# Backward chain of a recurrent-memory attention block: row products in four blocks of 112 columns

## The chip, the cores and the metric

The kernel runs on one core of a Trainium2 chip. A core has a matrix engine (PE in the profile, with weight loads shown apart as PEld), a vector engine (DVE), an activation engine (ACT), a general engine (POOL), a queue processor that issues transfers (SP) and 16 DMA engines. PE works on an array of 128 rows by 128 columns; a matmul of fewer weight columns uses a group of columns, so four matmuls of 32 weight columns can be in the array at once. The metric is the device time of one execution, in microseconds (us); it is given as the median of several runs.

## What is computed

A block with a recurrent memory: LayerNorm, attention over 64 segments one after the other, a residual, LayerNorm, SwGLU feed-forward, a residual. S = 2048 rows, D = 448, 16 heads of 256, 8 memory rows, segments of 32 rows, feed-forward width 1792. The outputs are the result and the gradients of all inputs.

```python
def _A_ref(x, mem0, Wq, Wk, Wv, Wo, seg_len):
    mem = mem0
    for s in range(n_seg):
        h = jnp.concatenate([mem, x[:, s * seg_len:(s + 1) * seg_len]], axis=1)
        q, k, v = (jnp.einsum('btd,dhe->bhte', h, W) for W in (Wq, Wk, Wv))
        scores = jnp.where(mask, jnp.einsum('bhqe,bhke->bhqk', q, k) * scale, -1e9)
        o = jnp.einsum('bhqk,bhke->bhqe', softmax(scores), v)
        o = jnp.einsum('bhte,hed->btd', o, Wo)
        mem = o[:, :M]
        outs.append(o[:, M:])
    return jnp.concatenate(outs, axis=1)

h = x + _A_ref(_layernorm(x), mem0, Wq, Wk, Wv, Wo)
out = h + (silu(_layernorm(h) @ w_gate) * (_layernorm(h) @ w_up)) @ w_down
# and the gradients of out with respect to every input, for a given grad_out
```

A segment has 40 rows: 32 of its own, and 8 memory rows that come from the segment before. The kernel holds them in this order, the memory rows last. In the gradient the order turns round: segment 63 comes first, and the gradient of a segment's memory rows has to be added into the output gradient of the segment before it, so the 64 backward segments are one chain.

## The kernel before

There are four stages: the forward chain (64 segments), the feed-forward with its gradient, the backward chain (64 segments, last first), and a tail that makes the weight gradients from arrays stored on the way. Rows are kept in 16 tiles of 128, that is of four segments each; r is a segment's place in its tile, and the backward chain runs r = 3, 2, 1, 0. The change is in the backward chain, with some preparation in the forward chain.

One backward segment does the following on PE. Line numbers are those of the kernel before.

- Output gradient (L1236): 16 heads of 256 are 32 column blocks of 128. For each, four matmuls over D (padded to 512) with a 128x128 block of WoT as weights and the 40 rows of output gradient as the moving operand: 128 matmuls. They are evicted to doT (heads in partitions), and 16 transposes (L1245) make dO_sb, rows in partitions.
- Gradients of the attention weights (scores, L1254): 32 matmuls of doT with the stored v, which SP loads by a transposing DMA (vT, L1153). DVE turns them into the score gradients dS_bd (prod, L1261 to L1267).
- Value gradient: head_mm (L1213) with dO_sb and the stored probabilities P_bd; then the same helper for k with the stored Q_sb, and for q with K_sb and the turned score gradients (L1304). Q_sb and K_sb are loaded for each segment by eight DMAs on SP (L1163).
- Each of these results is split in its eviction. The first 8 of a segment's own rows go to lo, which gathers them over a tile's four segments: no later segment needs them. The other 32 rows (24 own rows and the 8 memory rows) go to blk.
- Row products (rows_in, L1293): for v, k and q, 32 matmuls each of a 128x32 block of blk with 448 columns of WvT, WkT or WqT. The 32 columns of weights take a quarter of the array, and the j-th block goes to column group j mod 4, so the sum stands in four parts in pH.
- The four parts are added (L1322): DVE copies pH to omb in float32 (L1319), and eight float matmuls with a selection matrix sel give the sum, turned. Its last eight columns go into do_roll (L1326), which the next segment's L1236 reads. The other 24 are staged for the LayerNorm gradient (L1338 and others).
- Between these steps L1378 fills PE: 96 more row products for each tile, over the first rows in lo. In r=3 they are finished with L1385 (the sum over the four groups) and L1393 (four float transposes), and the LayerNorm gradient (ln_bwd, L253 to L264) is taken straight from PSUM.

The program is written for a scheduler that keeps each engine's instructions by priority; `k.prio.crit()` raises the chain above the rest, and `tc.issue_after(x)` holds an instruction behind another on its engine. Results in PSUM come from pools with rotating buffers: five psf banks, two fx, and one po. All loads of the chain are on SP, and most stores on POOL. Near the chain's end parts of the weight gradients and the loads for the tail (k.tl, rows_of_blocks, memory_rows) are prepared too; the last two are DMAs on POOL.

Of the kernel before, what the change touches and what calls it, by code (L numbers as in the profile page):

```python
# [15 lines left out]
P = 128  # L16
# [129 lines left out]
def run_all(k: _K):  # L146
# [19 lines left out]
    k.ps1 = lambda: psum.tile([P, 512], FP32, tag="ps", name="psf", bufs=5)  # L166
    k.fx1 = lambda: psum.tile([P, 512], FP32, tag="fx", name="fx", bufs=2)
    k.po1 = lambda: psum.tile([P, 512], FP32, tag="po", name="po", bufs=1)
    k.ph1 = lambda: psum.tile([P, 1024], BF16, tag="po", name="ph", bufs=1)
# [34 lines left out]
    def dt(name, shape, dtype=BF16):  # L204
# [7 lines left out]
              X_o=dt("X_o", [NB, P, MC * P]), HC=dt("HC", [NB * P, DP]), Oh=dt("Oh", [S, D]),  # L212
              DC0=dt("DC0", [P, 4, D]), DC1=dt("DC1", [P, NB - 4, D]))
# [101 lines left out]
class _TailLoads:  # L315
# [28 lines left out]
    def rows_of_blocks(self, i):  # L344
        k, D, S, NT, M, SEG = self.k, self.k.D, self.k.S, self.k.NT, self.k.M, self.k.SEG
        pool, DHb, DC0, DC1 = k.nc.gpsimd, k.dr["DHb"], k.dr["DC0"], k.dr["DC1"]
        if i < 4:
            dcx = DHb[0:S, 0:D].rearrange("(t r i) d -> r i t d", r=4, i=SEG)[i, M:SEG]
            pool.dma_start(out=DC0[32 * i:32 * i + 24], in_=dcx[:, 0:4])
            pool.dma_start(out=DC1[32 * i:32 * i + 24, 0:NT - 4], in_=dcx[:, 4:NT])  # L350
        else:
            g = i - 4
            pool.dma_start(out=DC1[:, NT - 4 + g, :], in_=DHb[0:S, 0:D].rearrange("(g s i) d -> g s i d", s=16, i=SEG)[g, :, 0:M])

    def memory_rows(self, g, rows):
        k, D, M = self.k, self.k.D, self.k.M
        for q in range(4):
            t = 4 * g + q
            dst = k.dr["DC0"][:, t] if t < 4 else k.dr["DC1"][:, t - 4]
            k.nc.gpsimd.dma_start(out=dst.rearrange("(r i) d -> r i d", r=4)[:, 24:32, :], in_=rows[32 * q:32 * q + 32, 0:D])  # L360
# [9 lines left out]
def forward_chain(k: _K):  # L370
# [280 lines left out]
    for s in range(NSEG):  # L651
# [166 lines left out]
        if s == 0:  # L818
            stats(2, NT, to_v.ins)
        nc.gpsimd.dma_start(out=oh[s, M:SEG, 0:256], in_=om2[0:24, :])  # L820
# [4 lines left out]
        for g in range(2):  # L825
            v_out = nc.sync.dma_start(out=dr["VG"][s, L * g:L * g + L], in_=Vs[64 * g:64 * g + L, :])
        if not end:
            rest_rows(s + 1)
# [61 lines left out]
def ffn_phase(k: _K, back):  # L890
# [32 lines left out]
    for i in range(2):  # L923
        nc.gpsimd.memset(dhb_b[i][:, D:DP], 0.0)
# [88 lines left out]
    for n, gi in enumerate(turns):  # L1013
# [67 lines left out]
        for tt in range(G):  # L1081
# [16 lines left out]
            nc.scalar.copy(out=dh_b[:, 0:D], in_=dh_t)  # L1098
# [10 lines left out]
def backward_chain(k: _K):  # L1109
# [3 lines left out]
    ident, dr, sel = k.ident, k.dr, k.sel  # L1113
# [3 lines left out]
    NWIN = 8  # L1117

    WoT_sb = W(0, KC, HD)
# [5 lines left out]
    dxT = B(7, 1024).bitcast(FP32).rearrange("p (c n) -> p c n", n=P)  # L1125
    vT = A(49.5, 16, 2 * L)
    dO_sb = A(52, 16, P)
    doT = A(56, 32, 64)
    do_roll = A(60, KC, NWIN, L)
    xn_t = B(9, D)  # L1130
    dh_h = [B(9.875, 448).bitcast(FP32), A(48.5, 448).bitcast(FP32)]
    dx3 = A(48, KC * 48).bitcast(FP32).rearrange("p (c n) -> p c n", c=KC)
    lq3 = k.mv2[:].rearrange("p t n -> p (t n)").bitcast(BF16).rearrange("p (c m) -> p c m", m=M)
    dx2 = [(A(64.5, 96).bitcast(FP32).rearrange("p (c n) -> p c n", c=2), 0, 2, P, 2),
           (A(48.375, 48).bitcast(FP32).rearrange("p (c n) -> p c n", c=1), 2, 3, P, 2),
           (k.maskb[:, 0:24].unsqueeze(1), 3, 4, 64, 2)]
    dx1 = B(4.375, KC * 48).bitcast(FP32).rearrange("p (c n) -> p c n", c=KC)
    dx_stage = [(dx3, 0, KC, P, 3)] + dx2 + [(dx1, 0, KC, P, 1)]
    dhx = A(62.5, KC, P)
    dmr = A(63.5, KC, 16, M)  # L1140
    P_bd, dS_bd, dST_bd = [B(1.25 * i, 8, 2, L) for i in range(3)]
    Pb = [B(3.75, 8, L)]

    def prep_tile(t):
# [4 lines left out]
        for kc in range(KC):  # L1149
            nc.gpsimd.tensor_copy(out=do_roll[:, kc, s0:s0 + 4, 0:SEG], in_=dhx[:, kc, :].rearrange("p (g j) -> p g j", g=4))  # L1150
# [4 lines left out]
    def load_seg(s):  # L1155
        if s < NSEG - 1:
            load_v(s)
# [6 lines left out]
        P_sb = Pb[0]  # L1164
# [22 lines left out]
    load_seg(NSEG - 1)  # L1187
# [458 lines left out]
```

## Time and profile before

| | us |
|---|---|
| median of three runs (2927.2 to 2939.27) | 2931.01 |
| the profiled execution | 2921.87 |
| its span in the profile | 2920.1 |
| forward chain and what begins of the feed-forward, 0 to 975 | 975: PE busy 903, DMA share 0.76 |
| feed-forward, 975 to 1257 | 282: PE busy 277, DMA share 0.92 |
| backward chain, 1257.5 to 2253 | 995: PE busy 979, DMA share 0.55 |
| tail, 2253 to 2920 | 667: PE busy 647, DMA share 0.81 |
| one backward segment, r = 2, 1, 0 | 14.88 |
| one backward segment, r = 3 | 17.2 |
| first interval of the chain | 23.45 |

A matmul's row in the profile has its own latency in it (an L1236 matmul lasts 179 ns, while they start every 25 ns), so the number of a kind times its mean is no time on PE; the distance of the starts is. The median lies 9 us above the profiled execution, 0.3%.

### The profile page before, as it was taken

Reading aid. Unit: us, or ns where it says so; the run is one execution under the profiler, and the core shown is the slowest. Engines: PE = TensorE matmul, PEld = TensorE weight load, DVE = VectorE, ACT = ScalarE, POOL = GpSimd, SP = SyncE. Lnnn points to the kernel's source line nnn. Section 1 sums busy time; section 2 is a strip of 40 time slices with the busy share of each in tenths; the row PEclk is TensorE's granted clock in tenths of the full one; section 3 lists DMA queues with packets and bytes.
Section 4 is the critical chain, followed back from the end, with each engine's and each line's share of the span. In section 5 each row is a group of like instructions: output and inputs, shape, how many; then the busy total and the mean of one; then the engine's idle time right before and its main releaser. Section 6 shows DMA issues by size and latency. Waiting matters only on the chain.

```text
span 2920.1 us, 108265 instructions
## 1 busy us (share of the span) xinstructions
PE 2805.9 (96%) x47650; PEld 1746.3 (60%) x47650; DVE 1328.6 (45%) x3320; ACT 1077.0 (37%) x2590; POOL 704.1 (24%) x1676
## 2 busy tenths in 40 slices
PE   4999999999999999989999999999999989999998
PEld 3555565555555555667777777677766544545444
DVE  4555565556455666745555555555554011111110
ACT  2554454455454454433333333343333011111110
POOL 1222232233222222422222222222222111212211
PEclk9999999999999999999999999999999999999999
DMA  7577777777778988985555555555555998969941
GB/s 258 152 193 192 192 193 195 192 194 200 198 185 229 285 219 215 257 259 151 142 145 154 144 141 155 137 148 149 142 154 170 347 269 175 207 183 238 207 147 52
DMA packets 743132, 552.14 MB, mean 189 GB/s; under 512 B 601796, under 2 KB 639060, under 8 KB 740100
## 3 DMA queue, kind: packets, MB, share of 16 engines
q1 hardware_dynamic: 692788, 402.38, 55.9%
q0 software_dynamic: 49872, 142.83, 14.4%
q8 instruction: 374, 6.13, 0.9%
q14 instruction: 98, 0.80, 0.1%
HBM read 169.84 MB, written 236.13 MB: 139 GB/s over the span
## 4 chain that ended last, share of the span: by engine, by line
PE 80%; issue 8%; DMA 4%; ACT 3%; DVE 2%; POOL 2%; SPq 0%; POOLq 0%; ACTq 0%; DVEq 0%
PE po L1293 11%; PE psf L1487 8%; PE psf L1236 7%; PE psf L569 6%; PE psf L704 5%; PE psf L1213 5%; PE psf L967 4%; PE po L751 4%; PE fx L1378 3%; PE fx L1487 3%; PE fx L1091 3%; PE psf L593 2%; PE psf L1322 2%; PE psf L1245 2%; PE psf L485 2%
## 5 line engine op out<-in xcount | busy, mean ns | idle before, releaser
L76 ACT CAST arA<-psf 128x384 bf16<-128x384 f32 (+6 forms) x1083 | 419.8, 428 | 845.0 <-PE psf L1487 215.1
L75 DVE CAST arA<-psf 128x256 bf16<-128x256 f32 (+6 forms) x797 | 358.4, 471 | 687.8 <-PE psf L1487 248.9
L1293 PE MATMUL po<-arW,arA 128*32 128x448 bf16 x6144 | 328.1, 355 | 5.6 <-DMA arW<-Tq 4.1
L1487 PEld LDWEIGHTS <-arA 128*128 128x128 bf16 x1440 | 139.0, 98 | 160.6 <-issue 4.8
L1236 PEld LDWEIGHTS <-arW 128*128 128x128 bf16 x8192 | 211.2, 96 | 23.3 <-issue 18.4
L1487 PE MATMUL psf<-arW,arA 128*128 128x512 bf16 x882 | 222.7, 381 | 0.0
L1293 PEld LDWEIGHTS <-arA 128*32 128x32 bf16 x6144 | 146.8, 96 | 120.3 <-ACT arA L76 9.3
L1236 PE MATMUL psf<-arA,arW 128*128 128x40 bf16 x8192 | 217.2, 180 | 0.8 <-DVE arA L1326 0.8
L704 PE MATMUL psf<-arW,arA 128*64 128x512 bf16 x1536 | 212.1, 382 | 0.0
L569 PE MATMUL psf<-arW,arA 128*32 128x512 bf16 x3072 | 189.8, 381 | 7.7 <-DVE arA L75 0.9
L76 ACT COPY arA<-psf 128x512 bf16<-128x512 bf16 (+3 forms) x206 | 142.9, 727 | 39.5 <-PE psf L593 24.0
L76 ACT CAST arB<-psf 128x64 bf16<-128x64 f32 (+1 forms) x320 | 107.7, 337 | 135.1 <-PE psf L576 73.6
L967 PE MATMUL psf<-arW 128*128 128x256 bf16 (+1 forms) x1288 | 149.0, 277 | 5.0 <-DVE arA L75 3.7
L75 DVE COPY arA<-psf 128x512 bf16<-128x512 bf16 (+2 forms) x204 | 104.3, 512 | 99.5 <-PE psf L1245 82.4
L967 PEld LDWEIGHTS <-arW 128*128 128x128 bf16 (+1 forms) x1344 | 103.2, 97 | 56.9 <-issue 45.4
L569 PEld LDWEIGHTS <-arA 128*32 128x32 bf16 x3072 | 70.3, 96 | 105.1 <-issue 28.8
L751 PE MATMUL po<-arW,arA 128*32 128x256 bf16 (+1 forms) x4096 | 126.9, 261 | 1.2 <-DVE arA L75 1.2
L1564 POOL DMA_DIRECT2D out_dram<-arA x96 | 52.2, 544 | 262.0 <-DVE arA L75 233.6
L1527 PE MATMUL psf<-arW 128*128 128x448 bf16 x525 | 111.6, 352 | 3.0 <-DVE arA L75 1.6
L1213 PEld LDWEIGHTS <-arW 128*128 128x128 bf16 x2048 | 79.5, 99 | 49.6 <-issue 48.1
L751 PEld LDWEIGHTS <-arA 128*32 128x32 bf16 x4096 | 104.0, 96 | 8.5 <-DVE arA L75 1.5
L1168 POOL COPY arB<-arB 40x320 bf16<-40x320 bf16 x128 | 58.9, 460 | 174.8 <-DMA arB<-P_all 86.7
(298 smaller groups left out, 4553.5 us busy)
## 6 DMA issues: line engine op xcount, KB each, us to landing
arW<-T SPq DMA_DIRECT2D x256, 128.0 KB
X_o<-arA SPq DMA_DIRECT2D x37, 512.0 KB
T<-arA SPq DMA_DIRECT2D x64, 256.0 KB
X_v<-arA POOLq DMA_DIRECT2D x30, 512.0 KB, 4.9
X_k<-arA POOLq DMA_DIRECT2D x30, 512.0 KB, 4.7
X_q<-arA POOLq DMA_DIRECT2D x30, 512.0 KB, 4.1
out_dram<-arA POOLq DMA_DIRECT2D x84, 128.0 KB, 3.8
VG<-arA SPq DMA_DIRECT2D x64, 160.0 KB
```

Of the source, the lines that this page charges most:

```text
L75: return nc.vector.tensor_copy(out=out, in_=in_)
L76: return nc.scalar.copy(out=out, in_=in_)
L569: nc.tensor.matmul(banks[b][w][32 * q:32 * q + 32, :], lhsT=hT_roll[:, kc, sl, M:L], rhs=(Wq_sb, Wk_sb)[w][:, kc, col(q, b)], start=(b == ...
L704: nc.tensor.matmul(pV[b][64 * g:64 * g + 64, 0:512], lhsT=hT_flat[:, kc, sl * L:sl * L + 64], rhs=Wv_sb[:, kc, n * 512:(n + 1) * 512], sta ...
L751: last = nc.tensor.matmul(pO[32 * q:32 * q + 32, 0:w], lhsT=xblk[:, j, r * SEG:(r + 1) * SEG], rhs=Wo_sb[:, cj(j), 256 * dh:256 * dh + w], ...
L967: nc.tensor.matmul(ps[fp][:, f2 * 256:(f2 + 1) * 256], lhsT=Wt[lo:hi, kc, c * P:(c + 1) * P], rhs=xT[lo:hi, kc, :], start=(kc == 0 and f2 ...
L1091: k.last_dh = nc.tensor.matmul(pdh[:, 0:D], lhsT=srcT[:, tt, c, :], rhs=WT[:, c, :], start=(i == 0), stop=(i == 2 * FC - 1))
L1213: nc.tensor.matmul(ps[b][:, i * 2 * L:(i + 1) * 2 * L], lhsT=lhs[:, at, :], rhs=rhs_bd[:, cl // 2, :, :].rearrange("p g n -> p (g n)"), st ...
L1236: nc.tensor.matmul(pss[b][:, jj * L:(jj + 1) * L], lhsT=WoT_sb[:, kc, c * P:(c + 1) * P], rhs=do_roll[:, kc, sl, :], start=(kc == 0), stop ...
L1293: nc.tensor.matmul(pH[32 * (j % 4):32 * (j % 4) + 32, 0:D], lhsT=blk[nm][:, j, r * SEG:(r + 1) * SEG], rhs=WT[:, cj(j), :], start=(nm == " ...
L1487: k.last_mm = nc.tensor.matmul(pa[i][:, 0:w], lhsT=lhs_of(b)[:, i // 2 * P:(i // 2 + 1) * P], rhs=rhs_of(q, b, i % 2), start=(b == 0), sto ...
L1527: k.last_mm = nc.tensor.matmul(pa[i][:, 0:D], lhsT=lhs_of(b, i), rhs=rhs_of(b), start=(bi == 0), stop=(bi == m + 3))
```

## The change

In the backward chain, rows are multiplied with 112 columns at a time: D = 448 is four blocks of 112. Line numbers in this section are of the changed kernel.

- Row products (rows_in, L1322): every block of blk is used as weights four times, once in each column group q, with columns 112q to 112q+111. The four quarters of the array hold the complete sums of the four column blocks, in 112 columns of pH; nothing is added afterwards. One transpose (L1503) gives do_roll its memory rows. The products over the first rows (rest_parts) take the same form.
- Output gradient (grads_by_col, L1182): the last 32 rows of a segment's output gradient (24 own rows and the 8 memory rows) are the weights now, 112x32 for each block of D, and 512 columns of WoT are the moving operand, four column groups at a time: 32 matmuls. WoT is held in blocks of 112 rows for it. The first 8 rows of a tile's four segments come from the feed-forward and not from the chain; they are done together, once a tile, with 32 more such matmuls, in r=2 and r=1 of the tile processed before it; the result is turned into R4 and stored to RO in HBM, from where each segment loads its part (load_rest). POOL copies it from R4 into doT.
- Value gradient: value_rest (K of 32 rows, in three row groups) and value_own (K of 128), each eight matmuls 160 wide, replace head_mm for v. They need the probabilities in another order: four stores a segment on SP put the first rows' part into PR during the forward chain (PR is filled with zeros once, by one DMA of 2.6 MB, L838), and seven loads a segment bring P4r and P4.
- LayerNorm input: ACT copies pH to dxs (L1500), and SP stores it to DXQ; the first rows go to DXR. Two tiles later norm_load brings both back in 11 DMAs for each tile, with the LayerNorm's other operands, and norm_first and norm_second (in r=3 and r=2) take the gradient.
- rows_of_blocks and memory_rows write or read a row in four pieces of 112 columns, 48 and 64 DMAs instead of 12 and 16, on SP instead of POOL.
- PSUM banks are named (k.bank) in place of rotating buffers in the chain.

SP's issues in a backward tile go from about 40 to 95. The diff, cut to its core:

```diff
+              RO=dt("RO", [NT, P, 1024]), PR=dt("PR", [NSEG, 4 * M, 16 * L]),
+              DXQ=dt("DXQ", [NSEG, P, D // 4], FP32), DXR=dt("DXR", [NT, P, D // 4], FP32),
...
+            blank = A(20, 2560)
+            nc.gpsimd.memset(blank, 0.0)
+            nc.sync.dma_start(out=dr["PR"].rearrange("s q n -> (s q n)").rearrange("(p a n) -> p a n", p=P, n=2560),
+                              in_=blank.unsqueeze(1).to_broadcast([P, 4, 2560]))
...
+        pr = dr["PR"][s].rearrange("(q k) (i c n) -> q k i c n", q=4, i=4, c=4)
+        for q in range(4):
+            g, x = divmod(q, 2)
+            nc.sync.dma_start(out=pr[q, :, :, 2 * x + g, :], in_=P_sb[64 * g:64 * g + M, 4 * x:4 * x + 4, :])
...
-        for kc in range(KC):
-            nc.gpsimd.tensor_copy(out=do_roll[:, kc, s0:s0 + 4, 0:SEG], in_=dhx[:, kc, :].rearrange("p (g j) -> p g j", g=4))
+        for c in range(4):
+            nc.gpsimd.tensor_copy(out=do_roll[0:DQ, c, s0:s0 + 4, 0:SEG], in_=dhx[0:DQ, c, :].rearrange("p (g j) -> p g j", g=4))
+        nc.gpsimd.tensor_copy(out=hRo[0:DQ].rearrange("p k (g j) -> p k g j", j=M), in_=do_roll[0:DQ, :, s0:s0 + 4, 0:M])
...
+    def grads_by_col(lhs, bank, b, c0=0, c1=4):
+        for c in range(c0, c1):
+            for q in range(4):
+                n0 = 1024 * q + 512 * b
+                last = nc.tensor.matmul(bank[32 * q:32 * q + 32, :], lhsT=lhs(c), rhs=WoT_sb[0:DQ, c, n0:n0 + 512],
+                                        start=(c == 0), stop=(c == 3), skip_group_check=True)
+        return last
...
+    def load_rest(s):
+        t, r = divmod(s, 4)
+        src = dr["RO"][t].rearrange("(q r k) (m e) -> r q k m e", q=4, k=M, e=P)
+        for w in range(3):
+            n = (3, 3, 2)[w]
+            nc.sync.dma_start(out=dOr[32 * w:32 * w + 32, 0:n], in_=src[r][:, :, 3 * w:3 * w + n])
+
+    def load_p(s):
+        pa = dr["P_all"][s].rearrange("p (x i n) -> p x i n", x=2, n=L)
+        for w in range(3):
+            nc.sync.dma_start(out=P4r[32 * w:32 * w + 32].rearrange("p i c n -> p (i c n)"), in_=dr["PR"][s])
+        for q in range(4):
+            g, x = divmod(q, 2)
+            nc.sync.dma_start(out=P4[32 * q:32 * q + 32, :, 2 * x + g, :], in_=pa[64 * g + M:64 * g + L, x])
...
+    def value_rest(ps):
+        for m in (0, 3, 6, 1, 4, 7, 2, 5):
+            w, a = divmod(m, 3)
+            last = nc.tensor.matmul(v_out(ps, m), lhsT=dOr[32 * w:32 * w + 32, a, :], rhs=p_rows(P4r[32 * w:32 * w + 32], m),
+                                    start=(a == 0), stop=False, skip_group_check=True)
+        return last
+
+    def value_own(ps, m0, m1):
+        for m in range(m0, m1):
+            last = nc.tensor.matmul(v_out(ps, m), lhsT=dO_own[:, m * P:(m + 1) * P], rhs=p_rows(P4, m),
+                                    start=False, stop=True, skip_group_check=True)
...
+    def rows_in(ps, lhs, WT, js, start=False, stop=False):
+        js = list(js)
+        for i, j in enumerate(js):
+            for q in range(4):
+                last = nc.tensor.matmul(ps[32 * q:32 * q + 32, 0:DQ], lhsT=lhs(j), rhs=WT[:, cj(j), DQ * q:DQ * q + DQ],
+                                        start=(start and i == 0), stop=(stop and i == len(js) - 1), skip_group_check=True)
+        return last
...
+    def rest_out(t):
+        nc.scalar.copy(out=pxs, in_=pX[:, 0:DQ])
+        nc.sync.dma_start(out=dr["DXR"][t], in_=pxs)
...
+    def norm_load(t):
+        x = norm[t] = [k.f32("f3", D, "dx"), None]
+        own = dr["DXQ"][4 * t:4 * t + 4].rearrange("r (q n) d -> r n q d", q=4)
+        rest = dr["DXR"][t].rearrange("(q r n) d -> r n q d", q=4, n=M)
+        for r in range(4):
+            x4 = x[0][:].rearrange("p (q d) -> p q d", q=4)
+            nc.sync.dma_start(out=x4[32 * r + M:32 * r + 32], in_=own[r, 0:24])
+            nc.sync.dma_start(out=x4[32 * r:32 * r + M], in_=rest[r])
...
+        if s < NSEG - 1:
+            nc.sync.dma_start(out=dr["DXQ"][s + 1], in_=dxs)
+            if r == 3 and t + 2 < NT:
+                norm_load(t + 2)
+            load_rest(s)
+            load_p(s)
+            load_v(s)
+            load_qk(s)
+        if r == 3:
             prep_tile(t - 1)
...
-            pss = [k.ps1() for _ in range(4)]
-            for j in range(MC):
-                c = cj(j)
-                b, jj = divmod(j, 8)
-                for kc in range(KC):
-                    with tc.issue_after(k.last_dh.ins) if s == NSEG - 1 and j == 0 and kc == 0 else nullcontext():
-                        nc.tensor.matmul(pss[b][:, jj * L:(jj + 1) * L], lhsT=WoT_sb[:, kc, c * P:(c + 1) * P],
-                                         rhs=do_roll[:, kc, sl, :], start=(kc == 0), stop=(kc == KC - 1))
-            for b in range(4):
...
+            own = [k.bank(0), k.bank(1)]
+            for b in range(2):
+                with tc.issue_after(k.last_dh.ins) if s == NSEG - 1 and b == 0 else nullcontext():
+                    grads_by_col(lambda c: do_roll[0:DQ, c, sl, M:L], own[b], b)
+            for b in range(2):
+                k.evac(dO_own[:, 512 * b:512 * b + 512], own[b][:], "vs"[b])
+            nc.gpsimd.tensor_copy(out=doT[:, :, 0:M], in_=R4_b[t % 2][:, :, r * M:(r + 1) * M])
+            pV = [k.bank(2 + b) for b in range(3)]
+            value_rest(pV)
+            grads_turned(k.bank(0), dO_own[:, 0:512], doT[:, :, M:L], 0)
+            value_own(pV, 0, 4)
+            last_t, turned_v = grads_turned(k.bank(1), dO_own[:, 512:], doT[:, :, M:L], 1)
...
+            if r in (0, 1) and t > 0:
+                with tc.issue_after(last_d.ins):
+                    last_t, _ = grads_turned(k.bank(0), rO, R4_b[(t - 1) % 2], 1 - r)
+                rest_saved(t - 1, 1 - r, rO)
...
-            k.last_om = nc.vector.tensor_copy(out=om[:, 0:D], in_=pH[:, 0:D])
-            pm = k.ps1()
-            for kc in range(KC):
-                nc.tensor.matmul(pm[:, kc * 32:(kc + 1) * 32], lhsT=om[:, kc * P:(kc + 1) * P], rhs=sel[:],
-                                 start=True, stop=True)
...
+            with tc.issue_after(last_q.ins):
+                rows_in(pH, lambda j: blk["k"][:, j, r * SEG:(r + 1) * SEG], WkT_sb, range(MC))
+            last_r = rows_in(pH, lambda j: blk["q"][:, j, r * SEG:(r + 1) * SEG], WqT_sb, range(MC), stop=True)
...
+            with tc.issue_after(last_r.ins):
+                if r in (2, 1) and t > 0:
+                    pR = pD
+                    grads_by_col(rest_lhs, pR, 2 - r, 0, 2)
+                else:
+                    rest_parts(FILL)
+            nc.scalar.copy(out=ot, in_=pH[:, 0:DQ])
+            nc.scalar.copy(out=dxs, in_=pH[:, 0:DQ])
...
+                pm = k.bank(2)[:].bitcast(BF16)
+                to_d = nc.tensor.transpose(pm[0:DQ, 0:P], ot, ident[:, :])
+                nc.vector.tensor_copy(out=do_roll[0:DQ, :, (s - 1) % NWIN, SEG:L],
+                                      in_=pm[0:DQ, 0:P].rearrange("p (c n) -> p c n", n=32)[:, :, 24:32])
+                with tc.issue_after(to_d.ins):
+                    if r in (2, 1) and t > 0:
+                        grads_by_col(rest_lhs, pR, 2 - r, 2, 4)
+                        k.evac(rO, pR[:], "s")
+                    else:
+                        rest_parts(FILL)
...
+            if r in (3, 2) and t + 2 < NT:
+                with tc.issue_after(cast["v"].ins):
+                    (norm_first if r == 3 else norm_second)(t + 2)
...
-            px = k.fx1()
-            for wi, (nm, WT) in enumerate((("q", WqT_sb), ("k", WkT_sb), ("v", WvT_sb))):
-                for j in range(MC):
-                    nc.tensor.matmul(px[32 * (j % 4):32 * (j % 4) + 32, 0:D], lhsT=lo[nm][:, j, :], rhs=WT[:, cj(j), :],
-                                     start=(wi == 0 and j < 4), stop=(wi == 2 and j >= MC - 4), skip_group_check=True)
-            om2 = k.f32("f3", D, "om2")
...
-            pX = k.fx1()
-            for kc in range(KC):
-                nc.tensor.transpose(pX[:, kc * P:(kc + 1) * P], dxT[:, kc, :], k.identf[:, :])
...
+    nc.sync.dma_start(out=dr["DXQ"][0], in_=dxs)
+    norm_load(1)
+    norm_first(1)
+    norm_second(1)
+    rest_parts(len(parts))
+    rest_out(0)
+    norm_load(0)
+    norm_first(0)
+    norm_second(0)
```

## The prediction

> **What bounds the kernel now.** I read the page from the top, then the windows by stage and by tile, then the timeline of one segment, then the waits and the timeline of SP.
>
> ```profile
> PE 2805.9 (96%) x47650; PEld 1746.3 (60%) x47650; DVE 1328.6 (45%) x3320; ACT 1077.0 (37%) x2590; POOL 704.1 (24%) x1676
> ...
> q8 instruction: 374, 6.13, 0.9%
> ...
> PE 80%; issue 8%; DMA 4%; ACT 3%; DVE 2%; POOL 2%; SPq 0%; POOLq 0%; ACTq 0%; DVEq 0%
> ```
>
> PE is busy for 96% of the span and the chain that ends last runs through it.
>
> ```profile
> 1257.50:2253.00 995.50, 978.53 (x23637) 707.03 (x23635) 515.74 (x1254) 379.85 (x1079) 232.77 (x578) 0.99 0.55 152
> ...
> 1541.08:1602.92 61.84, 61.45 (x1488) 44.39 (x1484) 32.35 (x79) 23.83 (x68) 14.08 (x36) 1.00 0.50 148
> ```
>
> The columns are the stretch, then busy time and count of PE, PEld, DVE, ACT and POOL, the granted clock, the DMA share and GB/s. The first row is the backward chain, the second one tile of four segments: 61.45 of 61.84 us are PE. Three segments of a tile take 14.88 us from first L1236 to first L1236; r=3 takes 17.2. Whatever leaves PE there comes off the time, as long as nothing else is late.
>
> ```profile
> 1603.09 3.37 PE L1236 MATMUL psf<-arA,arW 128*128 128x40 bf16 x128
> ...
> 1606.30 1.12 PE L1245 MATMUL psf<-ident,arA 128*128 128x128 bf16 x16
> ...
> 1607.35 0.69 PE L1254 MATMUL psf<-arA 128*64 128x40 bf16 x32
> ...
> 1608.07 0.75 PE L1213 MATMUL psf<-arB,arA 128*128 128x80 bf16 x16
> ...
> 1609.02 1.70 PE L1293 MATMUL po<-arW,arA 128*32 128x448 bf16 x32
> ...
> 1611.37 0.38 PE L1304 MATMUL psf<-ident,arB 128*40 128x40 bf16 x16
> ...
> 1613.09 2.64 PE L1293 MATMUL po<-arW,arA 128*32 128x448 bf16 x52
> ```
>
> A row's time is that of its whole group. Less the duration of one (354 ns for L1293, 179 for L1236, 187 for L1254, 181 for L1304), over the gaps, it gives start to start: 25 ns in L1236, 16 in L1254 (64 weight columns, so two column groups), 13 in L1304 (40 columns, two groups). L1293's 52 are 13 sets of four column groups: (2.64-0.35)/12 = 190 ns a set. One row of the forward chain's timeline:
>
> ```profile
> 640.81 1.48 PE L569 MATMUL psf<-arW,arA 128*32 128x512 bf16 x24
> ```
>
> Six sets of 512 columns, (1.48-0.38)/5 = 218 to 220 ns a set.
>
> **The change, part by part.** Everything up to the sum is PE time of one segment.
>
> *Row products.* A set becomes four matmuls of 112 columns, one for each column group. By the two rows above a set costs its columns at 0.43 ns and next to nothing else: 190-336x0.43 = 45 ns, or 112/2.4 = 47 and the 2 to 3 ns by which 190 exceeds 448/2.4. I take 49. 96 sets are 4.7 us, where the three L1293 groups start to start (1.65, 0.68, 2.28) are 4.6. The cost of such a set is in no row: from below 45; from above four times L1254's 16 ns = 65, or four times L1236's 25 = 101. I take 49 because the shape is L1293's, where the four of a set start 3 to 4 ns apart.
>
> One rule speaks against this. The Trainium skill ("TensorE: Matmul & The Clock Gate", Back-to-back issue gap) gives about 25 ns as a floor from one matmul to the next however few columns it has; the 384 would then take 9.6 us. The 13 ns of L1304 lies below that floor, so in this trace it can at most hold for each column group, not for each instruction; by the rule the segment would gain nothing.
>
> *Output gradient.* 128 L1236 matmuls (1603.09 to 1606.28, 3.2 us) become 32 of 512 columns, 8 sets of 216: 1.73. The first eight rows of each segment, done once a tile, are another 32, 0.43 a segment, and 8 transposes, 0.12. Transposes of the own rows fall from 16 to 8 (1.07 to 0.50).
> *Value.* 16 L1213 (0.68) become 8 with K of 32 and 8 with K of 128, 160 wide: 0.35 and 0.55 (the 128x160 row of L666 has 69 ns). Scores stay at 0.71.
> *End of the segment.* L1322, the float sum over four row groups (1.01), and its omb copy go; one transpose of 60 ns comes.
> *First rows by tile.* 96 sets of 49 instead of 96 matmuls under L1378: 1.18 a segment, where L1378 took 1.86 with its waits.
> *Unchanged.* L1304 0.36, heads k 0.70 and q 0.68.
>
> Sum: 1.73+0.43+0.12+0.50+0.35+0.55+0.71+4.7+1.18+0.36+0.70+0.68+0.06 = 12.1 us. PE will also wait where it did not: for the two gradient evictions (0.69 on DVE, 0.59 on ACT, of which value_rest hides a part), for the turned ones (0.41 to 0.51), the value eviction and the ot copy. The work to hide these is shorter now; I take 0.9 us together (0.5 to 1.5). So 13.0 instead of 14.88 us, and in r=3 the extra 2.3 us (L1385, L1393 and the LayerNorm steps between them) go off PE, since the LayerNorm input comes by DMA two tiles later. A tile: 4x13.0 = 52 instead of 61.84. Over 16 tiles that is 154 us.
>
> *What SP pays.*
>
> ```profile
> SPq L1153 <- PE psf L1213: 341.1, 51, 9.7
> ...
> SPq L1163 <- PE psf L1304: 87.7, 47, 2.6
> ```
>
> ```profile
> 1608.08 2.09 SPq L1153 DMA_TRANSPOSE arA<-VG  x1
> ...
> 1611.47 0.30 SPq L1163 DMA_DIRECT2D arW<-T  x1
> 1611.82 0.32 SPq L1163 DMA_DIRECT2D arW<-T0q  x1
> ```
>
> In 1300 to 2200 SP spends over 400 us waiting for PE to free a buffer: it has slack now. A direct DMA occupies it for 0.30 to 0.40 us, a V transpose for 1.3 to 2.1. A tile had about 40 issues on SP and gets 95: for each segment 3 for the rest of the gradient, 3+4 for P rows, 1 V, 8 for q and k and one DXQ store, and for each tile 11 of the LayerNorm, 2 RO, 1 DXR and 1 dhx. 90x0.40+5x1.6 = 44 us of a 52 us tile. On average it fits. In r=3 it does not: the DXQ store waits for ACT's copy of dxs at the end of r=0, and in SP's order r=3's loads stand behind it, some behind the LayerNorm loads too. Behind that wait in about five tiles are V and q,k: V issued at once lands some 3.7 us later (its packets in the trace end 3.2 to 4.2 us after the issue begins), due 3.2 us into the segment, 0.5 us of PE. In two, three P loads come first: 1.7. In about six tiles the whole list does, with three LayerNorm loads, the rest rows and the P rows ahead of V (13 issues, 4.7 us, then V's 3.7, due at 3.2): 5.2 to 6.4. Together 6x5.8+5x0.5+2x1.7 = 41 us; from below 15 (half of the landing overlaps), from above 90 (every tile the long kind). The 16 memory_rows and 12 rows_of_blocks issues that leave POOL come four for one onto SP; they are in the long tiles. POOL is at 14 of 62 us and hides its copies of R4, some 0.5 us each like L1168's; uncovered they would be 0.5 us a segment, because the scores read them.
>
> *LayerNorm steps.* They are taken at nothing: DVE has 30 of 62 us free and ACT 38. norm_first waits on ACT and DVE for loads that SP issued at the start of r=3, and stands behind the last first_rows of that segment, some 10 us later. Behind it on ACT are the copies ot and dxs, and for ot waits PE's transpose and with it the next segment: were the loads later than that, each us of it would be one of PE, once a tile.
>
> *Ends.* First tile: rest gradients, eviction, RO to HBM and back before the first value_rest, about 5 us. Last tile: 80 rest parts, then DXR to HBM and back, with bank 3 held for the LayerNorm while the tail wants it: 8 (0 to 15). Forward: 256 PR stores are 100 us of SP, which is busy about half of that chain, but they wait for a 2.6 MB fill: 5 (0 to 10). DMA's share in the chain rises from 0.5 to about 0.7; landings get later, 6 us in all.
>
> Sum: 154-41-5-8-5-6 = 89 us off 2921.87, the time of the profiled execution: 2833. The median of the three runs, 2931, lies 0.3% above it; on that footing 2842.
>
> **The rivals.** (B) *SP sets the pace.* For it: 95 issues, and L1163 rows of 1.3 and 1.4 us stand among those of 0.3. At 0.55 a direct DMA a tile takes 90x0.55+8 = 57.5 and with 2.5 us of r=3 stall 60: 16x1.8 = 29 us gained, less the 24 of the ends and landings: 2926 on the median's footing, with 2885 to 2945 around it. Against it: the median of the L1163 rows is 0.30 to 0.33.
>
> (C) *PE's front sets the pace, and the kernel is slower.* A set of four is eight instructions in 49 ns, 163 a us, for stretches of 6 us (256 row products of k and q). The densest 0.5 us that I find in the trace is L1254's, 64 instructions, 127 a us; over 3 us it is 80, in L1236. Instructions arrive in packets of 16 KB (6.13 MB over 374), one for about 260 PE instructions, at least 3.3 us apart, each taking 0.9 to 1.5; the change wants one every 1.6 us. With 120 sets in each of 64 segments, each ns on a set is 7.7 us. At 65 ns (L1254) that is +123: 2965. At 101 (L1236) +399: 3241. It decides from 2842 to 2931, 12 ns: 61 ns a set. Against it: L1293's sets show loads and matmuls alternating 1.7 ns apart within a set, and L1304 150 a us for 0.2 us.
>
> (D) *The new waits eat it.* If PE's idle is 1.5 us a segment and SP's stalls 90: 38+49 us more than my case, 2929, about as before.
>
> **How the numbers follow.** My case has 0.53, 2795 to 2885: low with SP stalls of 15 and idle of 0.5 (26+26 us less, 2790), high with half of D. B has 0.15, C 0.25, D 0.07. Left out of the range should be 2 in 10: the dear part of C above 2955 (0.17) and a little below 2785, so 2785 to 2955. This kernel's measurement can tell about 0.5%, 15 us, from no change. Faster than 2916: all of my case and nearly half of B and D, 0.62. Within 15 us: the rest of B and D, 0.13. Slower: C, 0.25.
>
> **What would show it.** L1182 at 1.7 us in place of 3.2; the k and q row products (L1326) as 256 matmuls in 3.1 to 3.2 us: at 4.2 or more C holds. r=1 and r=2 at 12.6 to 13.4 us a segment. In r=3, PE waiting for DMA ahead of value_rest or the scores, 0.5 to 6 us; SP issue under 48 us a tile, otherwise B. Banks freed late would show as PE waits on ACT. Most wrong would be a price of SP's new shapes (128 pieces of 80 bytes in a P load) far from L1163's, or a set that costs over 60 ns.

## The result, and the profile after

The changed kernel takes 3447.39 us (median of four runs, 3435.63 to 3471.32) against 2930.38: 1.177 times the kernel before (interval 1.169 to 1.184). The prediction was 2842, with a range to 2955. The profiled execution took 3438.14 us, 516 more than the 2921.87 of before.

| stage, by first instructions on PE | before | after | difference |
|---|---|---|---|
| feed-forward's first matmul (L967, L991) | 955.0 | 980.9 | +26 |
| chain's first output gradient of own rows | 1257.6 | 1306.8 | +49, so 23 in between |
| tail's first matmul (L1527, L1679) | 2253.0 | 2756.7 | chain 995 to 1450 us: +454 |
| end of the span | 2920.1 | 3436.4 | tail 667 to 680 us: +13 |

So almost all of it is in the chain, whose segments take some 22 us instead of 14.88. From the page of the changed kernel, busy time of the engines, then the instruction queue (packets, MB, share), then the chain of waits:

```profile
PE 2831.1 (82%) x64027; PEld 1821.1 (53%) x64031; DVE 1290.5 (38%) x3287; ACT 1012.5 (29%) x2494; POOL 693.8 (20%) x1632
...
q8 instruction: 502, 8.22, 1.0%
...
PE 64%; issue 18%; DMA 7%; ACT 4%; SPq 3%; DVE 2%; POOL 1%; POOLq 0%; ACTq 0%; DVEq 0%
```

PE's share fell from 96% to 82% and "issue", time in which PE waited for nothing that the profile shows, rose from 8% to 18%. There were 374 instruction packets before, and 502 now. What PE waited for in the chain (total us, times, longest):

```profile
PE bank L1322 <- issue: 349.7, 207, 4.7
PE bank L1287 <- issue: 24.8, 14, 3.7
PE bank L1304 <- DMA arB<-PR: 16.5, 9, 7.8
PE bank L1412 <- DMA arA<-VG: 15.3, 10, 2.8
PE bank L1456 <- issue: 14.8, 7, 3.3
PE bank L1310 <- DMA arA<-P_all: 9.3, 7, 1.7
```

The row products L1322 wait 350 us for no other engine; the waits for SP's loads are small beside that. The PE timeline of one segment (start, us, then the idle time before it):

```profile
1850.87 3.18 PE L1322 MATMUL bank<-arW,arA 128*32 128x112 bf16 x128
...
1857.03 1.56 PE L1322 MATMUL bank<-arW,arA 128*32 128x112 bf16 x112
1860.37 1.76 PE L1322 MATMUL bank<-arW,arA 128*32 128x112 bf16 x128 [1.78 <-issue]
1864.67 1.31 PE L1322 MATMUL bank<-arW,arA 128*32 128x112 bf16 x48 [2.54 <-issue]
```

Read the second line by the prediction's method: (1.56-0.23)/27 = 49 ns a set, as forecast. At this pace, though, a stretch ends after some 128 pairs (a weight load and its matmul are a pair), and a gap of about 2 us follows. 128 pairs are 256 instructions, one packet of 16 KB: 502 packets of 256 are 128,512 instructions, and the page counts 128,058 loads and matmuls. The first line is something else: (3.18-0.3)/31 = 93 ns a set, nearly twice 49, with one matmul lasting 300 ns instead of 225. There PE runs at a lower clock: the granted clock is 0.50 from 1850.87 to 1853.80, and 1.00 from 1857.03 to 1858.50. The whole chain, by windows (columns as in the prediction):

```profile
1306.83:2756.70 1449.87, 988.63 (x40089) 759.79 (x40088) 472.37 (x1215) 315.10 (x984) 227.87 (x541) 0.89 0.48 123
```

The granted clock is 0.89 where it was 0.99 before: it stands at half for 305 of these 1450 us, against 10 of 995. Of 7,679 distances from one set of L1322 to the next, 6,263 are 40 to 60 ns and 968 are 85 to 110; 966 of the latter lie at half clock.

### The profile page after: what moved, and what is told of

The parts are those of the page before. It is cut to its first block, busy times and chain, and to the rows that moved or that the text cites. A ratio compares the mean times of both kernels' runs of the same rounds, so it can differ in the third digit from the quotient of the medians.

```text
span 3436.4 us, 142732 instructions
## 1 busy us (share of the span) xinstructions
PE 2831.1 (82%) x64027; PEld 1821.1 (53%) x64031; DVE 1290.5 (38%) x3287; ACT 1012.5 (29%) x2494; POOL 693.8 (20%) x1632
## 4 chain that ended last, share of the span: by engine, by line
PE 64%; issue 18%; DMA 7%; ACT 4%; SPq 3%; DVE 2%; POOL 1%; POOLq 0%; ACTq 0%; DVEq 0%
PE bank L1322 13%; PE psf L1639 7%; PE psf L585 5%; PE bank L1182 4%; PE po L767 3%; PE psf L991 3%; PE psf L720 3%; PE bank L1287 3%; PE fx L1115 2%; PE psf L609 2%; PE fx L1639 2%; ACT arA L76 2%; PE bank L1412 2%; DMA arA<-VG 1%; PE psf L501 1%
## 5 line engine op out<-in xcount | busy, mean ns | idle before, releaser
L1322 PE MATMUL bank<-arW,arA 128*32 128x112 bf16 x28672 | 463.3, 225 | 326.3 <-issue 326.0
L1322 PEld LDWEIGHTS <-arA 128*32 128x32 bf16 x28672 | 406.3, 103 | 373.5 <-issue 357.5
L76 ACT CAST arA<-psf 128x512 bf16<-128x512 f32 (+3 forms) x379 | 189.3, 508 | 531.3 <-PE psf L1639 215.2
L75 DVE CAST arA<-psf 128x512 bf16<-128x512 f32 (+2 forms) x285 | 159.8, 561 | 490.8 <-PE psf L1639 249.9
L76 ACT CAST arA<-bank 128x384 bf16<-128x384 f32 (+3 forms) x576 | 174.5, 365 | 175.1 <-PE bank L1310 134.4
L1182 PE MATMUL bank<-arW,arA 112*32 112x512 bf16 x2560 | 198.7, 447 | 15.3 <-issue 8.6
L991 PE MATMUL psf<-arW 128*128 128x256 bf16 (+1 forms) x1288 | 149.5, 275 | 2.9 <-DVE arA L1057 1.1
L75 DVE CAST arA<-bank 128x384 bf16<-128x384 f32 (+3 forms) x384 | 128.5, 393 | 34.9 <-PE bank L1287 33.6
L991 PEld LDWEIGHTS <-arW 128*128 128x128 bf16 (+1 forms) x1344 | 103.1, 97 | 55.4 <-issue 44.2
L1287 PE MATMUL bank<-arB,arW 128*128 128x80 bf16 x2048 | 104.8, 213 | 27.7 <-issue 24.8
L585 PEld LDWEIGHTS <-arA 128*32 128x32 bf16 x3072 | 70.3, 96 | 104.2 <-issue 28.0
L1679 PE MATMUL psf<-arW 128*128 128x448 bf16 x525 | 115.6, 361 | 11.2 <-ACT arA L76 4.3
L75 DVE CAST arB<-bank 40x320 bf16<-40x320 f32 (+2 forms) x192 | 55.4, 312 | 179.6 <-PE bank L1456 177.4
L1182 PEld LDWEIGHTS <-arA 112*32 112x32 bf16 x2560 | 74.4, 110 | 90.8 <-issue 51.8
```

Source lines behind the costliest of these rows:

```text
L75: return nc.vector.tensor_copy(out=out, in_=in_)
L76: return nc.scalar.copy(out=out, in_=in_)
L585: nc.tensor.matmul(banks[b][w][32 * q:32 * q + 32, :], lhsT=hT_roll[:, kc, sl, M:L], rhs=(Wq_sb, Wk_sb)[w][:, kc, col(q, b)], start=(b == ...
L991: nc.tensor.matmul(ps[fp][:, f2 * 256:(f2 + 1) * 256], lhsT=Wt[lo:hi, kc, c * P:(c + 1) * P], rhs=xT[lo:hi, kc, :], start=(kc == 0 and f2 ...
L1182: last = nc.tensor.matmul(bank[32 * q:32 * q + 32, :], lhsT=lhs(c), rhs=WoT_sb[0:DQ, c, n0:n0 + 512], start=(c == 0), stop=(c == 3), skip_ ...
L1287: last = nc.tensor.matmul(ps[b][:, i * 2 * L:(i + 1) * 2 * L], lhsT=lhs[:, at, :], rhs=rhs_bd[:, cl // 2, :, :].rearrange("p g n -> p (g n ...
```

## The experiments

All times are medians, with the ratio to the kernel before on the same chip and its interval.

**split4: narrow products alone, on the kernel before.**

```diff
-                for j in range(j0, j1):
-                    nc.tensor.matmul(pH[32 * (j % 4):32 * (j % 4) + 32, 0:D], ..., rhs=WT[:, cj(j), :], ...)
+                w = D // 4
+                for j4 in range(j0, j1, 4):
+                    for c in range(4):
+                        for j in range(j4, j4 + 4):
+                            nc.tensor.matmul(pH[32 * (j % 4):32 * (j % 4) + 32, w * c:w * c + w], ...,
+                                             rhs=WT[:, cj(j), w * c:w * c + w], ...)
```

> The kernel before, with each 448-column row product of the chain cut into four matmuls of 112 columns in the same column group: same result, same array time (four sets of 49 ns for one of 190), same queues, 288 more load-and-matmul pairs a segment. Theory supply (PE is fed in 16 KB packets of 256 instructions, one each 3.3 to 3.5 us at best): 658 pairs are 1316 instructions, 5.1 packets, 17 to 22 us a segment instead of 14.88, total 3100 to 3400 us. Rival SP queue and waits for DMA: no change there, 2915 to 2960 us.

Measured 3343.66 us, 1.140 (1.132 to 1.148): as supply forecast. Nothing on SP or on the other engines was changed, and the same array work in four times the instructions costs 411 us. PE's waits in the chain:

```profile
PE po L1296 <- issue: 206.2, 140, 4.7
PE psf L1213 <- issue: 31.6, 17, 5.3
```

The heads' products (L1213), which were not touched, wait too: whoever is next when a packet runs out. PE's waits under "issue" come to 268 us in all rows of this view. What the rest of the 411 is was not taken apart; the mean clock was 0.956 where it was 0.995.

**split2: two products of 224 columns.** The same edit with w = D // 2.

> The same with two matmuls of 224 columns: 466 pairs, 932 instructions, 3.6 packets a segment; a set of four lasts 98 ns, 82 instructions a us against a supply of 73 to 78. Theory supply: almost covered by the 14.88 us of a segment, 2930 to 3000 us. Rival SP queue: 2915 to 2960. A rival that each extra instruction costs a fixed time: a third of split4's loss.

Measured 2987.67, 1.017 (1.013 to 1.022), as supply forecast: 96 more pairs cost 55 us, 288 more cost 411. A fixed price for each instruction would have made it 137. So the first 96 pairs a segment are mostly covered, and the next 192 are not.

**bench: the disputed cost by itself.**

```python
def four(mm, b, n, sets, rhs):
    for i in range(sets):
        for q in range(4):
            mm(banks[b][32 * q:32 * q + 32, 0:n], lhsT=Wt[:, i % 16, 32 * q:32 * q + 32], rhs=rhs[:, 0:n], ...)
```

> The disputed cost by itself: PE alone on constant data, nothing of the model is computed. Sets of four column groups with 448, 112, 448, 224, 160 and 32 columns, then 1024 single 128x128 loads with 40 columns, all with no DMA traffic, and at the end 512 sets of 112 columns beside 32 loads of 1 MB. Theory supply: long runs of less than 104 ns for eight instructions can't be held: 112, 160 and 32 columns all cost 104 to 110 ns a set, 224 columns 100 to 106, 448 columns 190, the 40-column pairs 26 to 27 ns. If packets come late only because the queues are full of other transfers, 112 columns cost 49 ns a set without traffic and 104 or more beside it. If the sequencer itself is the limit, the cost is even, without gaps.

Stretches of its PE timeline. L147 (sets of 112 columns), L151 (224), L155 (32) and L159 (single group of 40) have idle transfer queues; L157 is sets of 112 again, beside 32 loads of 1 MB:

```profile
34.13 1.76 PE L147 MATMUL b<-X,Wt 128*32 128x112 bf16 x128 [1.39 <-issue]
37.86 1.76 PE L147 MATMUL b<-X,Wt 128*32 128x112 bf16 x128 [1.97 <-issue]
41.59 3.00 PE L147 MATMUL b<-X,Wt 128*32 128x112 bf16 x128 [1.97 <-issue]
45.04 1.83 PE L147 MATMUL b<-X,Wt 128*32 128x112 bf16 x128 [0.45 <-issue]
...
126.33 3.25 PE L151 MATMUL b<-X,Wt 128*32 128x224 bf16 x128 [0.20 <-issue]
130.06 3.25 PE L151 MATMUL b<-X,Wt 128*32 128x224 bf16 x128 [0.48 <-issue]
...
173.43 1.23 PE L155 MATMUL b<-X,Wt 128*32 128x32 bf16 x128 [2.54 <-issue]
176.88 1.23 PE L155 MATMUL b<-X,Wt 128*32 128x32 bf16 x128 [2.23 <-issue]
...
206.16 3.36 PE L159 MATMUL b<-X,Wt 128*128 128x40 bf16 x128 [0.37 <-issue]
210.16 3.35 PE L159 MATMUL b<-X,Wt 128*128 128x40 bf16 x128 [0.65 <-issue]
...
240.97 1.76 PE L157 MATMUL b<-Y,Wt 128*32 128x112 bf16 x128 [1.69 <-issue]
247.17 3.10 PE L157 MATMUL b<-Y,Wt 128*32 128x112 bf16 x128 [4.44 <-issue]
```

128 pairs come every 3.45 to 4.0 us (3.7 on average), then, beside the loads, every 6.2 us; once the loads are through it is 3.5 to 3.7 us again. The stretch at 41.59 lasts 3.00 us, since the clock stood at half, and the next one still comes 3.45 us after it.

What the gaps wait for can be read from the trace's records of the instruction packets. All 45 gaps of over 1 us in the bench (from one weight load to the next) ended 1.2 to 1.6 us after the transfer of such a packet had ended. In the chain of the changed kernel, where some of the 237 gaps of this length are waits for other loads, the middle half ended 1.3 to 1.5 us after one.

Start to start, a pair cost 27.7 ns with 112 columns, 26.9 with 224, 27.6 with 160, 28.3 with 32 and 29.1 in the single group of 40 columns: five kinds of matmul, whose array time differs up to sevenfold, at nearly one price. 448 columns cost 190 ns a set without a gap. A set of 112 costs 111 ns in a long run, and 167 beside the loads. So "49 without traffic" fell, and so did "an even cost": the stretches run at 49 ns and stop.

**wide: the changed kernel with 448-column products again.** The four row groups are added by bf16 matmuls.

```diff
-            for q in range(4):
-                last = nc.tensor.matmul(ps[32 * q:32 * q + 32, 0:DQ], lhsT=lhs(j), rhs=WT[:, cj(j), DQ * q:DQ * q + DQ], ...)
+            q = (i if len(js) > 1 else j) % 4
+            last = nc.tensor.matmul(ps[32 * q:32 * q + 32, 0:D], lhsT=lhs(j), rhs=WT[:, cj(j), :], ...)
...
+            nc.scalar.copy(out=o4[:, 0:224], in_=pH[:, 0:224])
+            nc.vector.tensor_copy(out=o4[:, 224:D], in_=pH[:, 224:D])
+            for c in range(4):
+                nc.tensor.matmul(pm[0:DQ, 8 * c:8 * c + 8], lhsT=o4[:, DQ * c:DQ * c + DQ], rhs=selb[:, 24:32], ...)
+            rows_sum(pS, o4)
```

> The changed kernel, with its row products (own rows and first rows) again 448 columns wide in one column group, and the sum over the four groups by bf16 matmuls with a selection matrix (8 small ones a segment); its output gradient, value gradient, SP queue and LayerNorm by DMA stay. 290 fewer pairs a segment. Theory supply: 13.0 to 13.7 us a segment and some 50 us of DMA waits in all, total 2850 to 2930 us. Rival SP queue: it has the same 95 issues a tile, so 3350 us and more.

Measured 3140.01, 1.072 (1.068 to 1.076): 307 us below the changed kernel, but 210 above the top of my forecast. The supply waits are gone (2.7 us in the last line), and what they had covered comes out:

```profile
PE bank L1307 <- DMA arB<-PR: 81.9, 21, 14.1
PE bank L1424 <- DMA arA<-VG: 33.0, 18, 3.4
PE bank L1313 <- DMA arA<-P_all: 27.9, 18, 2.5
...
PE bank L1290 <- issue: 2.7, 1, 2.7
```

From scores to scores most segments take 13.5 to 16.4 us; from r=0 to r=3 it is 22 to 35. SP's waits say why:

```profile
SPq L1396 <- ACT arA L1521: 92.0, 41, 7.5
SPq L1351 <- ACT arB L1350: 75.5, 14, 8.4
```

L1396 and L1351 are the DXQ and DXR stores. SP stands at a store whose data come at the end of a segment, with the next loads behind it.

**nonorm: the changed kernel without the LayerNorm gradient.** DXQ, DXR, their loads and the steps are taken out.

> The changed kernel without the LayerNorm gradient of the input (its stores, loads and steps are left out, so the first gradient output is not made): 17 to 20 fewer issues on SP a tile, the same PE instructions. Theory supply: 3380 to 3440 us, only part of the DMA waits goes. Rival SP queue: below 3250 us.

Measured 3367.95, 1.149 (1.140 to 1.157), 79 us less and a little below the span that supply gave; far above what the SP rival needs.

**wide2 and after_sp: another order on SP.**

```diff
-            nc.sync.dma_start(out=dr["DXQ"][s + 1], in_=dxs)
-            if r == 3 and t + 2 < NT:
-                norm_load(t + 2)
             load_rest(s)
             load_p(s)
             load_v(s)
             load_qk(s)
+            nc.sync.dma_start(out=dr["DXQ"][s + 1], in_=dxs)
+            if r == 2 and t + 2 < NT:
+                norm_load(t + 2)
```

> wide, with SP's order changed: a segment's loads are asked for ahead of the DXQ store, and the 11 LayerNorm loads of a tile (and its two steps) come one segment later, in r=2, behind r=3's loads. Same instructions. If the 9 to 20 us that each tile lost in wide between r=0 and r=3 are SP's loads standing behind the DXR round trip and the LayerNorm loads: 14 to 15.5 us there, total 2890 to 2980 us. If the transfers themselves are too slow, or the number of issues: no more than 40 us gained, 3100.

Measured 3184.11, 1.085 (1.083 to 1.087): worse than wide, a miss. Most of the stall moved: from the scores of r=2 to those of r=1 it is now mostly 22 to 26 us, since the RO store (L1198) stands among the LayerNorm loads, and SP waits for ACT's copy of rO:

```profile
SPq L1198 <- ACT prod L76: 156.5, 25, 10.0
```

From r=0 to r=3 it is still 16 to 30 us.

> The changed kernel with the same new order on SP, its 112-column row products kept. Theory supply sets the pace: the DMA waits of 46 us go at most, 3380 to 3450 us. If SP set the pace in the changed kernel: 3250 or less.

Measured 3395.70, 1.157 (1.155 to 1.160), as supply forecast.

**wide3 and after_q: the three stores on POOL.**

```diff
-        nc.sync.dma_start(out=dr["RO"][t][:, 512 * b:512 * b + 512], in_=src)
+        nc.gpsimd.dma_start(out=dr["RO"][t][:, 512 * b:512 * b + 512], in_=src)
...
-        nc.sync.dma_start(out=dr["DXR"][t], in_=pxs)
+        nc.gpsimd.dma_start(out=dr["DXR"][t], in_=pxs)
...
+        nc.gpsimd.dma_start(out=dr["DXQ"][s], in_=dxs)
```

> wide2 with the chain's three stores (DXQ, DXR, RO), which wait for copies at the end of a segment, on POOL's queue instead of SP's, so that no load on SP stands behind them. If it is these waits in front of the next segment's loads that made wide and wide2 lose 10 us and more at a place (in wide2 SP waits 157 us for RO's data and 76 us for DXR's): all segments at 13.4 to 15 us, total 2870 to 2930 us. If SP or the transfers are too slow for 13.5 us a segment: 3000 us or more.

Measured 2977.35, 1.015 (1.013 to 1.018): 207 us below wide2 for three stores on another queue. Not the 2870 to 2930 expected: r=2 and r=1 mostly take 15 to 18 us, the others mostly 13.5 to 16, and the chain is 985 us against 995 before, at a clock of 0.95:

```profile
1307.75:2292.50 984.75, 906.95 (x17553) 554.31 (x17546) 498.05 (x1279) 332.19 (x1000) 287.07 (x650) 0.95 0.69 178
```

> The changed kernel with the LayerNorm loads in r=2 and the three stores on POOL, its 112-column products kept: what is left over wide3 is the price of the instruction supply alone. Theory supply: 19 to 21 us a segment, 3300 to 3400 us. If the stores ahead of loads had been the main loss of the changed kernel: below 3100.

Measured 3388.47, 1.156 (1.152 to 1.159). The supply waits are back:

```profile
PE bank L1322 <- issue: 350.5, 205, 4.7
```

Against wide3, the same kernel but for the width of the products, their sum and the place where the first rows are finished, it is 411 us: the price of the narrow products, the same as on the kernel before (split4).

**wide4: LayerNorm loads and PR stores on POOL.** `norm_load(t + 2, nc.gpsimd)` in r=3, and `nc.gpsimd` for the PR stores.

> wide3 with the 11 LayerNorm loads of a tile on POOL's queue, and the forward chain's PR stores on POOL too (but segment 0's). If SP, with some 19 issues a segment, has no room left for 11 more in r=2 (there wide3 has 15 to 18 us between scores, 13.5 elsewhere): r=2 and r=1 fall to 13.5 to 14.5 us, 45 to 60 us less. If the forward chain's 20 us are the PR stores standing ahead of transposing loads on SP: the feed-forward starts at 955 to 962 us instead of 977. Both: 2900 to 2920 us, a little below the kernel before. If POOL's own issues, at 0.55 us each, take the place of the waits: 2950 to 3000 us.

Measured 3038.28, 1.035 (1.032 to 1.038), a miss. Only r=2 falls as expected, to 13.8 us; r=1 mostly takes 15 to 18 and r=0 17 to 25. PE now waits for ACT's copy of the row products (41 us in all), for ACT's eviction of the output gradient (35) and for DVE's score gradients (35). The LayerNorm steps, whose loads POOL now issues, stand on the same two engines; that they are the cause was not tested. The feed-forward begins at 974.5 us, where 955 to 962 was expected.

**wide5: LayerNorm spread over a tile.** Eight loads in r=2, three in r=1, the steps in r=0 and the next r=3.

> wide3 (stores on POOL, loads on SP) with the LayerNorm spread over a tile: eight loads in r=2, three in r=1, first step in r=0, second in the next tile's r=3, so that neither DVE nor ACT stands waiting for its loads and SP has no eleven loads in a row. If wide3's 15 to 18 us in r=2 and r=1 (13.5 elsewhere) are these: 13.5 to 15 us, 40 to 70 us less than wide3, 2905 to 2940 us. If SP has no room for them anywhere: 2960 us or more.

Measured 2974.35, 1.014 (1.011 to 1.017): no gain over wide3 that can be told. r=2 mostly falls to 13.8, r=1 stays at 15 to 17, and every sixteenth segment (memory_rows, now 16 issues on SP) takes 22 to 24.

> wide5 without the 256 PR stores of the forward chain (PR keeps its zeros, so the value gradient lacks the part of the first eight rows). If these stores cost the forward chain its 20 to 26 us: the feed-forward's first matmul at 950 to 960 us as in the kernel before (955), and 15 to 30 us less than wide5. If it is the zero fill or the banks: within 5 us of wide5.

nopr leaves out only the four PR stores in each forward segment. Measured 2955.78, 1.009 (1.006 to 1.013), 19 us less; the feed-forward begins at 967.3 instead of 978.9. So the stores cost about half of the forward chain's loss. What the other half is (zero fill, bank naming) was not tried.

**bfsum: the removed addition alone, on the kernel before.**

```diff
-            k.last_om = nc.vector.tensor_copy(out=om[:, 0:D], in_=pH[:, 0:D])
+            nc.vector.tensor_copy(out=om[:, 0:224], in_=pH[:, 0:224])
+            nc.scalar.copy(out=om[:, 224:D], in_=pH[:, 224:D])
...
-                nc.tensor.matmul(pm[...], lhsT=om[:, kc * P:(kc + 1) * P], rhs=sel[:], ...)
+                nc.tensor.matmul(pm[...], lhsT=om[:, kc * P:(kc + 1) * P], rhs=selb, ...)
```

> The kernel before, with one part of what the change is after done alone: the addition of the four row groups costs little, because the partial sums are copied to bf16 (half on DVE, half on ACT) and added by four bf16 matmuls with a bf16 selection matrix, in place of a float32 copy and eight float32 matmuls (1.0 us a segment). Instructions fall by eight a segment. If the change's gain from having nothing left to add is real once instructions are not multiplied for it: 0.8 us a segment, 2870 to 2895 us. If that time lay in other work's shadow: 2915 to 2940 us.

Measured 2923.49, 0.996 (0.994 to 0.998): faster than both kernels, but by 8 to 11 us and not by 50. PE timeline around the sum (L1381 are the fillers, L1238 the next segment):

```profile
1603.81 0.74 PE L1381 MATMUL fx<-arW,arA 128*32 128x448 bf16 x11
1604.49 0.19 PE L1325 MATMUL psf<-omb 128*128 128x32 bf16 x1
1604.61 0.55 PE L1381 MATMUL fx<-arW,arA 128*32 128x448 bf16 x5
1605.09 0.24 PE L1325 MATMUL psf<-omb 128*128 128x32 bf16 x3
```

r=2 and r=1 fall from 14.88 to 14.42 us; r=0 rises from 14.9 to 15.25, and r=3 falls from 17.2 to between 15.8 and 17.1. The sum's matmuls shrank by 0.7 us (start to next start, two rows of 0.1 to 0.2 us here for 1.0 before); such a segment now takes 28 fillers (4, 11, 5 and 8) where it took 24, and r=0 is left with 11 instead of 23. From the start of the second segment to that of the last, the profiled execution is 24 us shorter (932 against 956). But the chain's first interval takes 33.6 us instead of 23.45, with one wait of 14.8 us for DVE's score gradients, and the tail 678 instead of 667. Whether the edit causes these two was not tested.

## Why the prediction was wrong

*The failed step is the price of the row products*, "I take 49 because the shape is L1293's". 49 ns is right for a set within a stretch (6,263 sets in the trace, and the bench). It is not a price for 256 products one after another: PE is fed by packets of 256 instructions, and the bench gets one every 3.45 to 4.0 us. Fed like this a set costs 111 ns in a long run, and the own rows of a segment 96x111 = 10.7 us where I put 4.7. In the segment shown, 288 row products last from 1857.03 to 1865.98, 8.9 us; the prediction had named 4.2 us or more for 256 as rival C's sign. With 111 in place of 49 the prediction's sum gives 2842+62x7.7 = 3319. Of the 128 us left to 3447, the smaller terms below have some 44. How much of the rest is the clock, at half for 305 us of the chain, was not separated.

*The evidence had been read, and read the wrong way.* Rival C gave the packets, "at least 3.3 us apart", beside the one every 1.6 us that the change wants, and did not price itself from them. These 3.3 us were the floor: in the changed kernel, in split4 and split2 too, packets in the chain are never closer than 3.2 to 3.3 us, and the bench shows it with nothing else in the queues. 256 instructions over 3.3 us is 78 a us, and the kernel before's L1236, 128 pairs in 3.2 us, ran at that rate. Instead, rival C took L1254 and L1236 rows (65 to 101 ns a set, up to +399 us). Dividing once, some 627 pairs a segment (the trace's mean) into packets of 128, would have given 4.9 packets, at 3.4 us 16.7 us at the least: slower than 14.88 before any wait is counted. With that, C was the likeliest case, not one at 0.25.

*The rule from the Trainium skill* ("TensorE: Matmul & The Clock Gate", Back-to-back issue gap). I set it aside because of L1304's 13 ns. Within a stretch the bench agrees with me for several column groups: sets of four with 32 columns take 25 to 34 ns, under 9 a matmul. For a single group it agrees with the rule: with 40 columns, 917 of 1,023 distances from matmul to matmul are 25 ns. Over a long run it shows 27 to 29 ns a pair for both, close to the rule's 25, but by the packet and whatever the columns up to 224.

*What held.* The sum for a segment with the supply out of the way: 13.0 forecast, 13.47 in the undisturbed segments of wide3 (there with 448-column products and their sum). The waits for SP's loads in the changed kernel: 41 forecast, and the rows for PR, V and P loads above come to 16.5+15.3+9.3 = 41. But this was luck in part: PE was late itself. With PE fast (wide) the same list cost 143 us in these three. The prediction had seen that r=3's loads stand behind a store that waits, and put the stalls at 41 us. Once PE was fast, the DXQ and DXR stores held SP for some 168 us (wide), and moving three stores gave 207 us (wide2 to wide3), while SP's issues fell only from 95 to 88 a tile.

*Smaller terms.* Forward 5 forecast, 26 measured; between the forward chain and the first gradient nothing was forecast beyond the 5 us of the rest round trip, 23 measured; end 8 forecast, 13 measured. "The sum over four groups (1.01)" was counted in full: alone it was worth 0.46 us in r=2 and r=1, and 8 us in all. The 154 us of chain gain (16 tiles of 9.84 us are 157) became 11 us in wide3 (985 against 995). There PE's waits, for loads, DVE and ACT, come to 63 us and the clock was 0.95; the parts were not priced. One figure of rival C was off: 256 products at 49 ns a set last 3.1 us and not 6.

*Rivals B and D.* SP's issues take 56 us a tile in the changed kernel (a direct one 0.50 us on average, where 0.40 was put), above the 48 that the prediction had named as B's sign. Beside a tile of some 91 us they set no pace. In wide3 they are 50 us of a tile of 61; whether they bind there was not tested. D's waits came once PE was fast: 143 us for loads in wide, where D had 90.

## What to carry to other kernels

Count PE's instructions over each stretch of a few us, not only array time: divide them into packets of 256 and compare with the closest spacing of instruction packets that any trace shows. In this kernel, cutting a matmul into more column blocks was nearly free only while the average stayed near it: 224 columns (55 us) were at the edge and 112 (411 us) far beyond. A store that waits for the end of a stage does not belong on the queue that brings the next stage's loads. And an engine that becomes slow hides the waits of the others: price them as if it were fast before calling them small.

## What was not expected of the hardware

The supply is one packet at a time with a nearly fixed period: 3.45 to 4.0 us from one stretch to the next on idle queues, though the packet's own transfer takes about 1.0 us, and 6.2 us beside 1 MB loads. So transfers that no instruction waits for can slow PE by way of its instructions.

The granted clock fell to half in pieces of 3.4 us or a multiple, 59 of them in the chain of the changed kernel. On idle queues the bench's run of 112-column sets had two (41.8 to 45.2 and 79.4 to 86.2 us), with no gap longer than 2.3 us before them; most gaps of this length had none behind them. At half clock a set took 93 ns instead of 49, in the changed kernel, in split4 and in the bench, and one of L1182 427 instead of 216.
